# Opening of a fused attention and MoE kernel: order of the second head's rows, the transfers and the second pair's preparation

## The chip, the cores and the metric

One core of a Trainium2 chip runs the whole program. The metric is device time in microseconds of that core for one execution. Engines: TensorE (PE in rows, its weight loads PEld), VectorE (DVE), ScalarE (ACT), GpSimd (POOL) and SyncE (SP, which here issues every transfer). Each runs its own list of instructions in the order in which the program emits them, and waits on semaphores for the others.

## The reference

Clustered attention, then two feed-forward layers. Only the attention matters here. Each query and key is assigned to the nearest of 16 centroids of its head (largest cosine), and a query attends only to the keys of its own cluster:

```python
q_assign = np.argmax(np.einsum('bhsd,hcd->bhsc', q_n, c_n), axis=-1)
k_assign = np.argmax(np.einsum('bhsd,hcd->bhsc', k_n, c_n), axis=-1)
mask = q_assign[:, :, :, None] == k_assign[:, :, None, :]
scores = np.where(mask, scale * np.matmul(q, k.transpose(0, 1, 3, 2)), -1000000000.0)
scores = scores - np.max(scores, axis=-1, keepdims=True)
attn = np.exp(scores)
attn = attn / (np.sum(attn, axis=-1, keepdims=True) + 1e-09)
x = np.matmul(attn, v)
```

Batch 2, 8 heads, 768 positions, 64 values per head, float32. Behind it stand `x @ w_in`, a leaky ReLU, `@ w_out`, a norm, a gated layer and `@ w_out`.

## The kernel before

Heads go in pairs, numbered pr = 0 to 7; a pair's 768 queries go in two halves, so there are 16 phases (ph) of six slots each, one slot for each tile of 128 keys. Slot 0 is the first with score products; negative slots are the opening. A table of events, filled by `plan`, gives each step a slot and an order number in it; `slot` emits the steps of a slot sorted by that number, and this emission order is the order on every engine. Ahead of the slots runs `setup`, whose steps are put in order by the string `CHAIN`: one letter is one step (`c`, `n` the norm chains of centroids and pair 0 on VectorE, `m` the cluster products, `a` scale and argmax, `d` and `o` transfers and one-hots, `v` the rests of pair 0, `w` a run of filler products that nobody reads, their numbers in `WARM`, `l` loads of pair 1, `q` and `t` its squares and their sums).

A pair is prepared in these steps. Loads of q and k twice, row-wise (`nat`) and transposed (`raw`). `prep_sq` on ScalarE and `prep_ss` give the sums of squares, for pairs 1 to 3 on GpSimd. `prep_norm` turns them into reciprocal norms by fourteen small VectorE instructions for pair 1, and for pair 2 mostly on GpSimd. `prep_sims` part 0 multiplies raw values with centroids (L396) and part 1 transposes the result (L406) into PSUM. `prep_scale` (L413, VectorE) reads it from there, and `prep_arg` finds the largest in five steps, the last of which writes one-hot columns `oh` (L435). `prep_oht` transposes these (L444) into the single PSUM buffer `ps_pr`, ScalarE copies them out (L445), and `prep_dma_oh` sends 16 rows for each head into `op1` (L488). `prep_hi` (ScalarE, L465) and `prep_lo` (L471, VectorE for pair 0, GpSimd else) split raw values into a rounded part and a rest in `stages`; `prep_dma_a` and `prep_dma_b` send these to the operands: `op1` rows 0 to 63 hold the rounded parts, 64 to 79 the one-hots (a factor of -2^60 on one side makes other clusters vanish), 80 to 127 and `op2` the rests and, in two rows, the negated maximum.

For pair 0, head 0's one-hot rows are made straight in place: `oht_direct(0)` (twelve small products, L456, two copies by ScalarE, L459 and L460); head 1's go by `prep_oht` and `prep_dma_oh(1)`, the first transfer of slot -12.

Every phase needs the row maxima first: `max_tile` (two products on `op1` rows 0 to 79, L507, into `ps_mx`, in phase 0 also `ps_pv`; one VectorE reduction, L511), six to a phase, three for each head. `max_split` (L516, L517, VectorE) splits and negates, `max_rows` (L532) transposes, ScalarE copies the rows into `op2` (L541). Then `st_tile` makes a score tile (L554 on `op1`, L555 on `op2`, exponential on ScalarE, L556) and `pv_tiles` multiplies with v and sums (L570, L584). PSUM buffers: three `ps_st`, one `ps_mx`, one `ps_pv`, one `ps_pr`; whoever takes a buffer again waits for its last reader, also for one emitted later on another engine.

Around the change the order is: phase 0's maxima in slots -12 to -7, pair 1's sims (part 0) at the end of slot -7, its rounding and norm chain in slot -6, sims part 1 in slot -4, scale in slot -1, argmax steps and phase 1's maxima in slots 0 to 4, its one-hot transposes in slot 4, pair 2's sims in slots 4 and 5, its scale in slot 6, and the maxima of pair 1's first phase (`max_tile(2, 0)`) from slot 7.

Of the kernel before, what the change touches and what calls it, by code (L numbers as in the profile page):

```python
# [12 lines left out]
AF = mybir.ActivationFunctionType  # L13
# [5 lines left out]
BIG = float(2.0 ** 60)  # L19
# [43 lines left out]
    "hi": ((-18, 2.5), (-18, 2.6)),  # L63
    "lo": ((-10, 4.5), (-9, 4.5)),
    "sims": ((-19, 8), (-16, 1.5)),
    "norm": tuple((-18, 9 + n / 100) for n in range(14)),
    "scale": ((-13, 5),),
    "arg": ((-12, 5), (-11, 5), (-10, 5), (-10, 5.1), (-9, 5)),
    "oht": ((-8, 2.6),),
# [13 lines left out]
STEADY = 20  # L83
# [3 lines left out]
WARM = (6, 10, 1, 1, 3)  # L87
# [63 lines left out]
WARMS = ((-4, 0.3, 2),)  # L151
CHAIN = "cccwccbbccccclcsscncncncnmnnnnmnnwnnnndllxlaaaxaaawxpvvowowqqtt"
# [29 lines left out]
class Attention:  # L182
# [46 lines left out]
    def setup(self):  # L229

        nc, C, H, D = self.nc, self.C, self.H, self.D
        n = H * C
# [3 lines left out]
        src = self.centroids.rearrange("h c d -> (h c) d")  # L236
# [20 lines left out]
        v = nc.vector  # L257
# [20 lines left out]
        for i in range(2):  # L278
# [19 lines left out]
            "o": [lambda: self.oht_direct(0), lambda: self.prep_oht(0)],  # L298
# [3 lines left out]
            "v": [lambda i=i: self.prep_lo(0, i) for i in range(2)],  # L302
# [144 lines left out]
    def oht_direct(self, h):  # L447

        nc, X = self.nc, self.T // 2
        ps = [b()[0:32].rearrange("p a b -> p (a b)") for b in (self.bk.mx, self.bk.pv)]  # L450
        cols = self.oh[0].rearrange("p x e c i g -> p x (e c) i g")
        for i in (1, 0):
            for g in range(2):
                for x in range(X):
                    t = g * X + x
                    nc.tensor.matmul(ps[i][:, t * 128:(t + 1) * 128], lhsT=cols[:, x, :, i, g], rhs=self.idr,  # L456
                                     start=True, stop=True)
        o1 = self.op1[h][64:80]
        nc.scalar.copy(out=o1[:, 1, :], in_=ps[1][:16, :self.S])  # L459
        nc.scalar.activation(out=o1[:, 0, :], in_=ps[0][:16, :self.S], func=AF.Identity, scale=-BIG)  # L460
# [16 lines left out]
    def prep_dma_b(self, h):  # L477
        pr, r = h // 2, 64 * (h % 2)
        o1, o2 = f(self.op1[h % 4]), f(self.op2[h % 4])
        st = f(self.stages[pr % 2])  # L480
        d = self.nc.sync.dma_start
        d(out=o1[80:128], in_=st[r:r + 48, 0:2])
        d(out=o2[0:64], in_=st[r:r + 64, 2:4])
        d(out=o2[66:82], in_=st[r + 48:r + 64, 0:2])
# [147 lines left out]
    def plan(self):  # L632
# [3 lines left out]
        def at(s, o, fn, *a):  # L636
            ev.setdefault(s, []).append((o, len(ev.get(s, [])), fn, a))
# [4 lines left out]
        for pr in range(self.NP):  # L642
# [9 lines left out]
            if pr == 0:  # L652
                at(-12, -2, self.prep_dma_oh, 1)
                at(-12, -1, self.prep_dma_b, 0)
                at(-12, 1, self.prep_dma_b, 1)
            elif pr == 1:
                at(-5, 12, self.prep_dma_a, h)
                at(-4, 12, self.prep_dma_a, h + 1)
                at(4, 2.8, self.prep_dma_oh, h)
                at(4, 2.8, self.prep_dma_oh, h + 1)  # L660
                at(4, 12, self.prep_dma_b, h)
                at(5, 12, self.prep_dma_b, h + 1)
            else:
                for e in range(2):
                    at(b - 12, 2.5, self.prep_dma_a, h + e)
                    at(b - 12, 2.5, self.prep_dma_oh, h + e)
                    at(b - 11 + e, 2.5, self.prep_dma_b, h + e)
        for ph in range(NF):
# [3 lines left out]
            for k, s in enumerate(slots):  # L672
                at(s, 2.7 if s in slots[:k] else 0.5 if s % 2 or s < 0 else 1.5 if s < STEADY else 1.01, self.max_tile, ph, k)
# [504 lines left out]
```

## Time and profile before

| | us |
|---|---|
| three timed runs | 868.97, 876.44, 876.71 |
| their median | 876.44 |
| profiled execution | 869.91 |
| its span | 868.0 |
| TensorE, VectorE, ScalarE, GpSimd busy | 835.7, 602.4, 327.7, 395.8 |
| mean granted TensorE clock (1.00 is 2.4 GHz) | 0.992 |

The span runs from the first to the last instruction of the profiled execution; the execution's own time is 1.91 longer. Times in rows count from the start of the span. "Busy" is the time in which an engine works on instructions; the text behind "<-" in square brackets is the idle time ahead of an instruction and what the profile takes for its releaser. Of a wait for several semaphores it names the last by its own reckoning; where that one had long been done, it was another, often a transfer.

### The profile page before, as it was taken

The numbers are of one execution on the slowest core, as the hardware profiler recorded it, in microseconds if no ns is written. First come the engines' busy times: TensorE is split into PE (matmuls) and PEld (weight loads), VectorE is DVE, ScalarE is ACT, GpSimd is POOL, SyncE is SP. The second block draws the span as 40 slices with busy tenths as digits, with TensorE's granted clock in tenths as the row PEclk, the third lists the DMA queues.
The fourth block names the chain that finished last, engine by engine and source line by source line (L and its number), as shares of the span: only waits on it lengthen the run. The fifth ranks groups of instructions, "written<-read, shape, count | busy, mean of one in ns | idle before, by whom it ended". The sixth has DMA issues, their size and how long they took to land.

```text
span 868.0 us, 11480 instructions
## 1 busy us (share of the span) xinstructions
PE 835.7 (96%) x4279; PEld 633.2 (73%) x4279; DVE 602.4 (69%) x924; ACT 327.7 (38%) x623; POOL 395.8 (46%) x349
## 2 busy tenths in 40 slices
PE   5898999999999999999999999999999999999998
PEld 3554666666655688887778888778888888888886
DVE  7857787786677448999899876987555555555523
ACT  4545565565444424333344334342222122122110
POOL 4652112211002616777777665444554554554511
PEclk9799999999999999999999999999999999999999
DMA  7878076347442202222221221000221221221012
GB/s 231 213 191 205 18 197 141 113 118 161 87 123 74 74 1 71 76 75 96 73 96 53 74 71 49 24 25 26 73 72 49 74 73 49 73 73 50 0 49 97
DMA packets 24279, 75.69 MB, mean 87 GB/s; under 512 B 3680, under 2 KB 4896, under 8 KB 24224
## 3 DMA queue, kind: packets, MB, share of 16 engines
q1 hardware_dynamic: 24224, 74.96, 30.1%
q8 instruction: 34, 0.56, 0.3%
q14 instruction: 21, 0.17, 0.1%
HBM read 51.46 MB, written 3.15 MB: 63 GB/s over the span
## 4 chain that ended last, share of the span: by engine, by line
PE 72%; DVE 19%; issue 3%; ACT 2%; POOL 1%; DMA 1%; SPq 0%; DVEq 0%; ACTq 0%; POOLq 0%
PE ps_st L829 24%; PE ps_mx L829 10%; PE ps_pv L829 9%; PE ps_pv L570 7%; PE ps_pr L829 5%; PE ps_mx L507 4%; DVE dec_a L808 3%; DVE mx L511 3%; PE ps_pv L584 3%; PE ps_st L554 3%; PE ps_st L555 3%; DVE x L936 2%; DVE dec_a L806 2%; PE ps_pr L613 1%; DVE dec_e L811 1%
## 5 line engine op out<-in xcount | busy, mean ns | idle before, releaser
L892 POOL TENSOR_TENSOR gl<-v,gh 128x512 fp32r<-128x512 f32 x68 | 93.5, 1375 | 104.1 <-ACT gh L891 102.8
L556 ACT ACTIVATE p<-ps_st 128x384 f32<-128x384 f32 x192 | 85.0, 494 | 106.5 <-PE ps_st L555 105.7
L511 DVE TENSOR_REDUCE mx<-ps_mx 128x1 f32<-128x768 f32 x93 | 88.7, 954 | 43.4 <-PE ps_mx L507 42.8
L891 ACT CAST gh<-v 128x512 fp32r<-128x512 f32 x68 | 42.3, 622 | 134.3 <-DVE v L888 79.9
L888 DVE TENSOR_TENSOR v<-ps_st,t 128x512 f32<-128x512 f32 x36 | 24.9, 691 | 85.4 <-PE ps_st L829 85.4
L630 POOL TENSOR_TENSOR x1l<-X,x1h 128x384 fp32r<-128x384 f32 x15 | 16.0, 1064 | 148.7 <-ACT x1h L627 145.1
L570 PE MATMUL ps_pv<-p,vnat 128*64 128x384 f32 x384 | 72.8, 500 | 0.0
L507 PE MATMUL ps_mx<-op 80*128 80x384 f32 x186 | 56.8, 387 | 12.4 <-DVE mx L511 11.9
L884 DVE SCALAR_TENSOR_TENSOR v<-v,alpha,t 128x512 f32<-128x512 f32 x45 | 46.9, 1043 | 30.7 <-ACT v L883 30.7
L554 PE MATMUL ps_st<-op 128*128 128x384 f32 x192 | 67.8, 353 | 0.0
L829 PE MATMUL ps_st<-x1h,stage 128*128 128x512 f32 x272 | 67.8, 390 | 0.0
L808 DVE SCALAR_TENSOR_TENSOR dec_a<-raw,dec_a 128x512 uint32<-128x512 uint32 x66 | 66.1, 1002 | 2.3
L555 PE MATMUL ps_st<-op 82*128 82x384 f32 x192 | 65.4, 341 | 0.0
L936 DVE TENSOR_TENSOR x<-ps_mx,x 128x1024 f32<-128x1024 f32 x36 | 43.8, 1218 | 31.1 <-PE ps_mx L829 31.1
L816 POOL TENSOR_TENSOR dec_a<-dec_a,woh 128x512 f32<-128x512 f32 x28 | 45.5, 1623 | 36.1 <-ACT woh L819 32.3
L507 PEld LDWEIGHTS ps_mx<-op 80*128 80x128 f32 x186 | 29.0, 192 | 43.2 <-DVE mx L511 21.8
L829 PEld LDWEIGHTS ps_st<-x1h,stage 128*128 128x128 f32 x272 | 50.8, 188 | 10.6 <-ACT x1h L978 0.2
L829 PE MATMUL ps_st<-x1h,wvh 128*128 128x512 f32 x144 | 56.1, 389 | 0.0
L829 PE MATMUL ps_st<-x1h,wvl 128*128 128x512 f32 x144 | 56.1, 389 | 0.0
L829 PE MATMUL ps_st<-x1h,wih 128*128 128x512 f32 x132 | 51.7, 391 | 0.0
L829 PE MATMUL ps_st<-x1h,wil 128*128 128x512 f32 x132 | 51.4, 389 | 0.0
L811 DVE TENSOR_SCALAR dec_e<-dec_a 128x512 uint32<-128x512 uint32 x66 | 48.7, 737 | 2.2
(253 smaller groups left out, 1988.2 us busy)
## 6 DMA issues: line engine op xcount, KB each, us to landing
raw<-in_moe_w_out_dram SPq DMA_DIRECT2D x28, 512.0 KB, 3.5
op<-stage SPq DMA_DIRECT2D x32, 384.0 KB, 5.5
raw<-in_moe_w_in_dram SPq DMA_DIRECT2D x15, 512.0 KB, 3.6
raw<-in_moe_w_val_dram SPq DMA_DIRECT2D x12, 512.0 KB, 3.5
raw<-in_moe_w_gate_dram SPq DMA_DIRECT2D x12, 512.0 KB, 3.4
op<-stage SPq DMA_DIRECT2D x16, 288.0 KB, 5.8
nat<-in_qn_dram SPq DMA_DIRECT2D x8, 384.0 KB, 4.9
nat<-in_kn_dram SPq DMA_DIRECT2D x8, 384.0 KB, 5.7
```

What stands on the lines that cost most here:

```text
L507: nc.tensor.matmul(ps[:, g, :self.HS], lhsT=o1[0:80, 0, t * 128:(t + 1) * 128], rhs=o1[0:80, 1, sl], start=True, stop=True)
L511: nc.vector.tensor_reduce(out=self.mx[ph][:, k:k + 1], in_=ps[:, :, :self.HS], op=ALU.max, axis=AX.XY)
L554: nc.tensor.matmul(ps, lhsT=o1[:, 1, ks], rhs=o1[:, 0, qs], start=True, stop=False)
L555: nc.tensor.matmul(ps, lhsT=o2[:, 1, ks], rhs=o2[:, 0, qs], start=False, stop=True)
L556: nc.scalar.activation(out=self.P[s][:, e], in_=ps, func=AF.Exp, scale=self.scale)
L570: nc.tensor.matmul(ps[64 * e:64 * e + 64], lhsT=self.vnat[ph // 2][:, e, t0 + y], rhs=P[y][:, e], start=t0 + y == 0, stop=t0 + y == T - 1)
L808: v.scalar_tensor_tensor(out=a, in0=top, scalar=0xC0000000, in1=a, op0=ALU.bitwise_and, op1=ALU.bitwise_or)
L811: v.tensor_scalar(out=e, in0=a, scalar1=0xFF800000, scalar2=None, op0=ALU.bitwise_and)
L829: self.nc.tensor.matmul(ps, lhsT=a, rhs=b, start=first and i == 0, stop=last and i == len(terms) - 1)
L884: nc.vector.scalar_tensor_tensor(out=v, in0=v, scalar=self.nalpha[:, a], in1=t, op0=ALU.mult, op1=ALU.add)
L892: nc.gpsimd.tensor_tensor(out=lo, in0=v, in1=f(hi), op=ALU.subtract)
L936: nc.vector.tensor_tensor(out=dst, in0=ps, in1=dst, op=ALU.add)
```

## The change

`CHAIN` puts two loads of pair 1 (instead of one) ahead of pair 0's operand transfers, moves one `v` (the rest of k, now `prep_lo(0, 1)` first) into the norm chain, adds `e` behind `d` (the two parts of `prep_dma_b` that need only the rest of k) and `f` behind the second `v` (the part that needs the rest of q), and puts the other two loads of pair 1 behind the one-hots. `oht_direct` is called for both heads, with 16 columns each; for head 1 it takes three `ps_st` buffers and `ps_pr` and four copies on ScalarE. `WARM` and `WARMS` give other filler products: 13 for 10, 3 for 1, and two in each of the slots -10 to -7 for two in slot -4. `SECOND`, the table of pair 1, moves rounding, sims, norm chain, scale, argmax and one-hot transposes to later slots (0 to 5); its transfers move accordingly. In phase 1 the maximum products stand behind the score products of their slot.

```diff
 SECOND = {
-    "hi": ((-18, 2.5), (-18, 2.6)),
+    "hi": ((-12, 4), (-11, 4)),
     "lo": ((-10, 4.5), (-9, 4.5)),
-    "sims": ((-19, 8), (-16, 1.5)),
-    "norm": tuple((-18, 9 + n / 100) for n in range(14)),
-    "scale": ((-13, 5),),
-    "arg": ((-12, 5), (-11, 5), (-10, 5), (-10, 5.1), (-9, 5)),
-    "oht": ((-8, 2.6),),
+    "sims": ((-12, 1.4), (-11, 1.7)),
+    "norm": tuple((-12, 9 + n / 100) for n in range(14)),
+    "scale": ((-11, 5),),
+    "arg": ((-10, 5), (-10, 5.1), (-9, 5), (-9, 5.1), (-8, 5)),
+    "oht": ((-7, 2.6),),
...
-WARM = (6, 10, 1, 1, 3)
+WARM = (6, 13, 1, 3, 3)
...
-WARMS = ((-4, 0.3, 2),)
-CHAIN = "cccwccbbcccccclcsscncncncnmnnnnmnnwnnnndllxlaaaxaaawxpvvowowqqtt"
+WARMS = ((-10, 0.3, 2), (-9, 0.3, 2), (-8, 0.3, 2), (-7, 0.3, 2))
+CHAIN = "cccwccbbcccccllcsscncncncnmnnnvnmnnwnnnndexaaaxaaawxwpvfowollqqtt"
...
+            "e": [lambda: [self.prep_dma_b(h, (0, 2)) for h in range(2)]],
+            "f": [lambda: [self.prep_dma_b(h, (1,)) for h in range(2)]],
-            "o": [lambda: self.oht_direct(0), lambda: self.prep_oht(0)],
+            "o": [lambda: self.oht_direct(0), lambda: self.oht_direct(1)],
...
-            "v": [lambda i=i: self.prep_lo(0, i) for i in range(2)],
+            "v": [lambda i=i: self.prep_lo(0, i) for i in (1, 0)],
...
     def oht_direct(self, h):
...
+        if h:
+            hi = [self.bk.st(), self.bk.pr()]
+            ps = [[self.bk.st(), self.bk.st()], hi]
+        else:
+            ps = [b().rearrange("p a b -> p (a b)") for b in (self.bk.mx, self.bk.pv)]
+            ps = [[b, b[:, self.HS:]] for b in ps]
...
-                    nc.tensor.matmul(ps[i][:, t * 128:(t + 1) * 128], lhsT=cols[:, x, :, i, g], rhs=self.idr,
-                                     start=True, stop=True)
+                    nc.tensor.matmul(ps[i][g][0:16, x * 128:(x + 1) * 128], lhsT=self.oh[0][:, x, h, :, i, g],
+                                     rhs=self.idr, start=True, stop=True)
...
-        nc.scalar.copy(out=o1[:, 1, :], in_=ps[1][:16, :self.S])
-        nc.scalar.activation(out=o1[:, 0, :], in_=ps[0][:16, :self.S], func=AF.Identity, scale=-BIG)
+        for i in (1, 0):
+            parts = [(ps[i][g][:16, :self.HS], o1[:, i, sl]) for g, sl in self.halves()] if h else \
+                [(ps[i][0][:16, :self.S], o1[:, i, :])]
+            for src, dst in parts:
+                if i:
+                    nc.scalar.copy(out=dst, in_=src)
+                else:
+                    nc.scalar.activation(out=dst, in_=src, func=AF.Identity, scale=-BIG)
...
-    def prep_dma_b(self, h):
+    def prep_dma_b(self, h, parts=(0, 1, 2)):
...
+        pairs = ((o1[80:128], st[r:r + 48, 0:2]), (o2[0:64], st[r:r + 64, 2:4]), (o2[66:82], st[r + 48:r + 64, 0:2]))
+        for i in parts:
+            self.nc.sync.dma_start(out=pairs[i][0], in_=pairs[i][1])
...
             if pr == 0:
-                at(-12, -2, self.prep_dma_oh, 1)
-                at(-12, -1, self.prep_dma_b, 0)
-                at(-12, 1, self.prep_dma_b, 1)
+                pass
             elif pr == 1:
-                at(-5, 12, self.prep_dma_a, h)
-                at(-4, 12, self.prep_dma_a, h + 1)
-                at(4, 2.8, self.prep_dma_oh, h)
-                at(4, 2.8, self.prep_dma_oh, h + 1)
-                at(4, 12, self.prep_dma_b, h)
-                at(5, 12, self.prep_dma_b, h + 1)
+                at(1, 12, self.prep_dma_a, h)
+                at(1, 12.1, self.prep_dma_a, h + 1)
+                at(5, 2.8, self.prep_dma_oh, h)
+                at(5, 2.8, self.prep_dma_oh, h + 1)
+                at(5, 12, self.prep_dma_b, h)
+                at(6, 12, self.prep_dma_b, h + 1)
...
-                at(s, 2.7 if s in slots[:k] else 0.5 if s % 2 or s < 0 else 1.5 if s < STEADY else 1.01, self.max_tile, ph, k)
+                at(s, 2.7 if s in slots[:k] else 0.5 if (s % 2 or s < 0) and ph != 1 else 1.5 if s < STEADY else 1.01, self.max_tile, ph, k)
```

In `SECOND` a slot is counted from 12: (-12, 1.4) is slot 0, (-7, 2.6) is slot 5.

## Rows read from the trace of the kernel before

**Rows 1.** Page, the chain that ended last: share of the span by engine

```profile
PE 72%; DVE 19%; issue 3%; ACT 2%; POOL 1%; DMA 1%; SPq 0%; DVEq 0%; ACTq 0%; POOLq 0%
```

**Rows 2.** Busy time by stretch; columns: us, engines' busy (instructions), clock, transfers

```profile
0.00:88.00 88.00, 69.36 (x407) 41.14 (x407) 63.58 (x144) 41.42 (x78) 39.93 (x106) 0.92 0.79 208
88.00:868.00 780.00, 766.33 (x3875) 592.07 (x3873) 538.79 (x780) 286.30 (x545) 355.83 (x243) 1.00 0.25 74
18.86:21.27 2.41, 0.00 (x0) 0.00 (x0) 1.44 (x4) 0.00 (x0) 2.02 (x7) 0.64 0.95 177
21.27:25.80 4.53, 4.48 (x18) 2.18 (x18) 3.27 (x6) 0.47 (x1) 2.49 (x6) 0.50 0.95 203
25.80:29.90 4.10, 4.10 (x14) 3.20 (x14) 3.08 (x15) 3.62 (x7) 0.00 (x0) 0.51 1.01 279
38.40:46.60 8.20, 7.53 (x43) 4.02 (x43) 5.70 (x12) 3.29 (x7) 7.00 (x14) 0.79 0.25 75
66.00:69.00 3.00, 1.00 (x10) 0.57 (x12) 2.52 (x5) 1.68 (x4) 1.45 (x3) 1.00 0.56 114
```

**Rows 3.** Timeline, TensorE, 21 to 29 us; columns: start, length, instructions

```profile
21.30 0.98 PE L507 MATMUL ps_pv<-op 80*128 80x384 f32 x2 [2.44 <-DVE mh L517]
...
24.27 1.51 PE L396 MATMUL ps_st<-raw,cb 128*32 128x384 f32 x8
...
27.63 0.67 PE L554 MATMUL ps_st<-op 128*128 128x384 f32 x1
...
28.74 0.52 PE L555 MATMUL ps_st<-op 82*128 82x384 f32 x1
```

**Rows 4.** Timeline and transfers issued, 17 to 18 us: KB each, us to landing

```profile
17.16 0.63 SPq L488 DMA_DIRECT2D op<-oht  x1
...
op<-oht SPq DMA_DIRECT2D x1, 96.0 KB, 4.1
```

**Rows 5.** Timeline, VectorE, 14 to 39 us

```profile
14.64 1.82 DVE L471 TENSOR_TENSOR stage<-raw,stage 128x768 fp32r<-128x768 f32 x2
...
17.23 0.96 DVE L511 TENSOR_REDUCE mx<-ps_mx 128x1 f32<-128x768 f32 x1 [0.76 <-PE ps_mx L507]
...
20.20 0.17 DVE L517 SCALAR_TENSOR_TENSOR mh<-mx,mh 128x3 fp32r<-128x3 f32 x1
...
25.65 0.17 DVE L337 TENSOR_SCALAR n_a<-ss 128x24 int32<-128x24 int32 x1
...
28.47 0.30 DVE L344 RECIPROCAL n_a<-n_y 128x24 f32<-128x24 f32 x1
...
35.74 1.73 DVE L517 SCALAR_TENSOR_TENSOR mh<-mx,mh 128x3 fp32r<-128x3 f32 x1
...
37.40 0.94 DVE L511 TENSOR_REDUCE mx<-ps_mx 128x1 f32<-128x768 f32 x1
```

**Rows 6.** Timeline, ScalarE, GpSimd and VectorE, 29 to 50 us

```profile
29.68 0.83 ACT L366 ACTIVATE nat<-nat 128x768 f32<-128x768 f32 x1
...
30.59 3.02 POOL L377 TENSOR_TENSOR nat<-nat 128x384 f32<-128x384 f32 x5 [6.44 <-ACT nat L366]
...
33.86 3.59 POOL L471 TENSOR_TENSOR stage<-raw,stage 128x768 fp32r<-128x768 f32 x2
...
48.11 0.23 POOL L328 TENSOR_TENSOR n_y<-n_y,n_a 128x24 f32<-128x24 f32 x1
...
49.22 0.56 DVE L413 TENSOR_TENSOR sims<-ps_pr,n_a 128x384 f32<-128x384 f32 x1
```

**Rows 7.** Timeline, 45 to 51 us, and transfers issued near 47 us

```profile
45.94 0.58 ACT L445 ACTIVATE oht<-ps_pr,ohs 128x384 fp32r<-128x384 f32 x1 [2.25 <-PE ps_pr L444]
...
47.56 0.52 PE L406 MATMUL ps_pr<-idf,simc 128*128 128x128 f32 x3
...
op<-oht SPq DMA_DIRECT2D x2, 96.0 KB, 3.1
...
50.93 0.61 PE L507 MATMUL ps_mx<-op 80*128 80x384 f32 x2
```

More of the change, by code (lines that the diff above doesn't have):

```diff
@@ L150 @@
 LATE = (1,2)
-WARMS = ((-4, 0.3, 2),)
-CHAIN = "cccwccbbccccclcsscncncncnmnnnnmnnwnnnndllxlaaaxaaawxpvvowowqqtt"
+WARMS = ((-10, 0.3, 2), (-9, 0.3, 2), (-8, 0.3, 2), (-7, 0.3, 2))
+CHAIN = "cccwccbbcccccllcsscncncncnmnnnvnmnnwnnnndexaaaxaaawxwpvfowollqqtt"
 LINE = 32
@@ L449, in oht_direct @@
         nc, X = self.nc, self.T // 2
-        ps = [b()[0:32].rearrange("p a b -> p (a b)") for b in (self.bk.mx, self.bk.pv)]
-        cols = self.oh[0].rearrange("p x e c i g -> p x (e c) i g")
+        if h:
[4 more added lines that the diff above has]
+            ps = [[b, b[:, self.HS:]] for b in ps]
         for i in (1, 0):
@@ L454, in oht_direct @@
                 for x in range(X):
-                    t = g * X + x
-                    nc.tensor.matmul(ps[i][:, t * 128:(t + 1) * 128], lhsT=cols[:, x, :, i, g], rhs=self.idr,
-                                     start=True, stop=True)
+                    nc.tensor.matmul(ps[i][g][0:16, x * 128:(x + 1) * 128], lhsT=self.oh[0][:, x, h, :, i, g],
+                                     rhs=self.idr, start=True, stop=True)
         o1 = self.op1[h][64:80]
-        nc.scalar.copy(out=o1[:, 1, :], in_=ps[1][:16, :self.S])
-        nc.scalar.activation(out=o1[:, 0, :], in_=ps[0][:16, :self.S], func=AF.Identity, scale=-BIG)
+        for i in (1, 0):
[6 more added lines that the diff above has]
+                    nc.scalar.activation(out=dst, in_=src, func=AF.Identity, scale=-BIG)
     def prep_hi(self, pr, i):
@@ L480, in prep_dma_b @@
         st = f(self.stages[pr % 2])
[L481 to L484, printed above, removed]
+        pairs = ((o1[80:128], st[r:r + 48, 0:2]), (o2[0:64], st[r:r + 64, 2:4]), (o2[66:82], st[r + 48:r + 64, 0:2]))
+        for i in parts:
+            self.nc.sync.dma_start(out=pairs[i][0], in_=pairs[i][1])
     def prep_dma_oh(self, h):
```

## The prediction

> **What bounds the kernel now.** I read the page first, its chain: TensorE carries 72% of it and VectorE 19% [rows 1]. Then the busy time by stretch. From 88 us on TensorE is busy 766.3 of 780 us at full clock; in the first 88 us it stands still for 18.6 us and the granted clock is 0.92 [rows 2]. The change touches the preparation of pairs 0 and 1, so its worth is read in the first 51 us. My mark is the first maximum product of pair 1, `max_tile(2, 0)`, at 50.93 us [rows 7]: behind it every engine but the transfer queue keeps its order, so what is won or lost by then is carried to the end.
>
> Next the timeline of the opening, engine by engine. TensorE has one hole, 18.86 to 21.27 [rows 2]. The profile names a vector instruction as the releaser of the product behind it [rows 3], but that product is the first that reads head 1, whose one-hot rows come by a transfer issued at 17.16 that lands 4.1 us later, at 21.26 [rows 4]: that is the true releaser. In and behind the hole the granted clock falls to 0.5, the 1.2 GHz level, and stays there to the end of the next two stretches, near 29.8 [rows 2]. In this slow time stand pair 1's cluster products (1.51 us) and two fillers, all ahead of the first score product at 27.63; the fourth ends at 29.26 [rows 3].
>
> VectorE has little rest meanwhile: reductions of 0.96, pair 1's norm chain (fourteen small instructions, 25.65 to 28.77, 3.1 us), then argmax steps between phase 1's reductions. One tiny instruction, the second half of a split, takes 1.73 us where 0.17 is usual: it starts while GpSimd holds one of two subtractions of 1.8 us (33.86 to 37.45). The reduction behind it, phase 1's fourth, ends at 38.34 [rows 5, 6]. GpSimd itself works nearly without a gap from 30.59 to 48.34 at pair 2's norms; only then VectorE finishes these and scales, 49.22 to 49.78 [rows 6].
>
> **The change part by part.** All sums run against the profiled execution: 869.91 us, a span of 868.0 and 1.91 around it. The timed runs are 868.97, 876.44 and 876.71; their median stands 6.53 above the profiled one.
>
> *Rest of k early.* One of two subtractions (1.82 for both [rows 5]) moves into pair 0's norm chain; the one-hots, at that chain's end, come 0.9 later. Four transfers (786 KB) now leave before q's rest is ready and two (786 KB) behind it. The 786 KB ahead of them had landed when the first reduction ran at 17.23 [rows 5]; the other 1.57 MB at the 203 GB/s seen behind the hole [rows 2] take 7.7 us, so all is there by 25.0 at the latest. The scores won't ask before 25.4 (below): covered, by little at worst. Pair 1's raw rows and the values go behind these six; they are needed from 26.3 on. I put the transfers at nothing; if the rate were a fifth lower, the scores would be up to 1.5 late, which the wait found below still covers.
>
> *Head 1 without a transfer.* The 2.41 us hole goes. TensorE gets six more fillers and twelve small products ahead of the first maximum tile in place of three transposes; ScalarE four half-row copies. Head 0 needs now only two of the four one-hot steps before its products start, which gives some of the 0.9 back. I take the first reduction as 0.8 late, 18.05 (bounds: nothing, and 1.8, the 0.9 twice). Four copies of at most 0.58 (a copy of 384 columns on 128 rows [rows 7]) have head 1's rows there before the fourth reduction. Six reductions of 0.96, two splits of 0.4 and gaps of 0.3: end at 24.9. Before, the norm chain began behind them at 25.65. Won so far: 0.75.
>
> *Pair 1 behind the first scores.* Between the last split and the scores stand only three small products and a short copy: first score product at 25.4, fourth ending at 26.3 against 29.26. Won: 3.0. The eight fillers stand in waits for reductions, at no cost there.
>
> *Where that goes.* VectorE did pair 1's norm chain while TensorE made the slow products. Now it idles from 24.9 until scores, cluster products (0.8, half of 1.51 at full clock) and a maximum tile are through, 27.7, and does the chain behind that reduction: reduction to 28.65, chain 3.1 and 0.5 for GpSimd beside it, 32.3; second reduction 33.25; 0.65 for the product and third to 34.9; the split meets GpSimd's subtractions as before, 37.3; fourth reduction 38.25. Before: 38.34 [rows 5]. The win is gone by here. Bounds of the 0.5: nothing, and 3.2, the whole of GpSimd's adds (30.59 to 33.8 before [rows 6]).
>
> A rule is weighed here. The row shows 1.73 for 0.17, but the same instruction at 20.20 took 0.17 beside GpSimd's adds [rows 5]. The Trainium skill, GPSIMD Engine Reference, section 1 Specifications, says that GpSimd shares its SBUF interfaces with VectorE and contends with instructions of two SBUF inputs, which most of the chain's are. By that rule for all of them the sum would be up to 2.7 higher, 874.8; by the row it is 872.1.
>
> *One-hot transposes of pair 1.* They move from slot 4 to slot 5, behind the sims transposes of pair 2. Both write `ps_pr`, of which there is one buffer, and pair 2's sims stay in it until VectorE's scale in slot 6. Before, the order was the other way round, and the scale at 49.22 held up nobody. TensorE gets there at 45.2: before, 9.74 us lay between the fourth reduction's end and the end of the same sims transposes (38.34 to 48.08 [rows 5, 7]); 1.1 of it were pair 1's transposes and copy (0.52, 0.58), and a clock of 0.79 over 8.2 us [rows 2] means 3.4 at half clock, 1.7 owed to it; 38.25 + 9.74 - 2.8. How early is the scale? ScalarE's squares of pair 2, behind the first scores, end at 29.35 (30.51 before). GpSimd's run of 17.75 then ends at 47.15; 0.25 for its wait on VectorE's argmax steps; VectorE's rest of the norms and the scale took 1.44 (48.34 to 49.78 [rows 6]): 48.8, 1.0 earlier than before. Then transposes 0.5, ScalarE's copy 0.6, and the transfer, 3.1 from issue to landing [rows 7]: 53.1. Behind the waiting transposes stand a score pair and a pv group; from the copy's end to the mark 4.4 us passed before, with these two and more in them [rows 7], so from 49.3 they are through by 53.1 too. Before, the transfer left at the copy's end, 46.5, and landed at 49.6, hidden by 1.3. The other transfers that leave later are needed at slot 12, some 20 us on.
>
> Sum at the mark: 53.1 - 50.93 = 2.2 late; 869.9 + 2.2 = 872.1.
>
> **The rivals.** *The win is kept* (faster). GpSimd comes through earlier, or TensorE doesn't wait for the scale. For it: TensorE gets to the transposes 2.9 ahead of before (45.2 against 48.08). Against: GpSimd's nearly gapless run [rows 6]. Time: 869.9 - 2.9 = 867.0.
>
> *Moved, not won* (no change). The scores start earlier, VectorE's chain takes it back, and TensorE comes so late to the transposes that the scale and the transfer are mostly covered: 869.9, within 1.
>
> *The clock* (slower). Two new waits of TensorE, for the norm chain (about 30.1 to 33.3) and for the scale (45.2 to 48.8), are longer than the 2.41 after which 0.5 was granted to 29.8 [rows 2]. It decides if both are answered like that. From 21.27 to 29.90 TensorE was busy 8.58 us at half clock, 4.3 owed to it; twice that, less a little that hides behind VectorE: 872.1 + 8 = 880. Against: from 66 to 69 TensorE was busy 1.0 of 3 us and kept its clock [rows 2]. The Trainium skill, TensorE: Matmul & The Clock Gate, section What's actually happening, has the slow clock as the default and activity as what releases it; by that rule this rival, with which the hole agrees and 66 to 69 doesn't.
>
> **How the numbers follow.** The wait behind the scale is an order that the code fixes; its size rests on GpSimd's measured run: 0.47. Kept win 0.20, moved 0.18, clock 0.15. The likeliest gives 872.1, its own range is 870 to 875 (the contention's bounds, a landing 0.6 off). Over the cases the range is 866 (the kept win, with 1 to spare) to 881 (the clock's case, likewise); it takes in most of the runs' own spread, by whose upper two the sum would be 878.7. Against the median of 876.44, faster by over 1% is below 867.7, slower above 885.2; 1% is about what a measurement of this kernel can tell. The first needs the kept win and an execution like the profiled one: 0.17. The second needs the clock's full price on an execution like the upper two: 0.05. Within 1%: 0.78.
>
> **What would show it.** Right: no hole before the fourth maximum tile; first score product near 25.4; VectorE idle to about 27.7, the norm chain behind phase 1's first reduction; the fourth reduction near 38; TensorE idle before the one-hot transposes (L444) until VectorE's scale (L413); the mark near 53. Wrong: L444 without that wait; a split of 0.2 in phase 1; GpSimd through before 46; or long stretches at 0.5 after 30, the clock's case.

## The result, and the profile after

The changed kernel takes 883.19 us (median of four executions, 879.65 to 885.44) against 874.88 for the kernel before, run beside it (median of four, 868.97 to 876.71). The ratio is 1.0113, with a 95% interval of 1.0068 to 1.0158: slower, by 8.3 us between the medians and by about 10 by the ratio. The forecast was 872.1 in a range of 866 to 881; it is wrong, on the slow side, and the number lies nearest to that of the rival called the clock. In one kernel further down (both orders mended, fewer fillers) a single execution took 1855.5 us; its ratio leaves it out. The profiled execution took 885.44 us with a span of 883.7. In the code after, the lines of [rows 3 to 7] stand two to ten lower: the maximum's product L507 is L517, its reduction L511 is L521, the norm chain is L333 to L346, scores L564 and L565, one-hot transposes L446, the scale L415.

Busy time by stretch of the kernel after, with the columns of [rows 2]:

```profile
0.00:88.00 88.00, 67.69 (x332) 40.17 (x334) 57.42 (x130) 35.64 (x67) 37.87 (x106) 0.83 0.63 170
12.00:14.00 2.00, 2.00 (x7) 1.52 (x6) 1.86 (x5) 0.00 (x0) 0.00 (x0) 1.00 0.98 226
29.90:46.80 16.90, 11.65 (x41) 6.75 (x38) 11.92 (x21) 6.39 (x11) 10.79 (x15) 0.50 0.44 123
46.80:57.00 10.20, 7.29 (x49) 3.81 (x47) 7.98 (x18) 4.04 (x9) 4.66 (x13) 1.00 0.00 0
57.00:63.90 6.90, 5.88 (x23) 2.50 (x23) 0.86 (x2) 1.56 (x3) 0.00 (x0) 0.51 0.39 79
81.00:87.60 6.60, 5.93 (x24) 3.72 (x26) 3.08 (x6) 3.17 (x6) 0.72 (x1) 0.50 0.80 165
88.00:883.70 795.70, 780.07 (x3971) 599.52 (x3967) 548.56 (x795) 292.97 (x559) 357.49 (x244) 1.00 0.26 76
```

All the loss lies in the first 88 us (the prediction meant to read it in the first 51): behind them the clock is full and TensorE busy 98% of the time, before and after, and VectorE's reductions of the row maxima, matched one by one, stand 15.2 us behind those of the kernel before at 100 us and 15.6 at the last one. What is new in this execution is three stretches at half clock (0.50, the 1.2 GHz level), 30.4 us in all; before there were 10.2 us near 20 to 30 and a shorter one near 40 to 44 [rows 2].

TensorE's timeline of the kernel after:

```profile
11.69 5.53 PE L314 MATMUL ps_st<-zero,idr 128*128 128x512 f32 x14
...
28.16 0.39 PE L564 MATMUL ps_st<-op 128*128 128x384 f32 x1
...
40.50 1.01 PE L517 MATMUL ps_mx<-op 80*128 80x384 f32 x2 [5.25 <-DVE mx L521]
...
58.02 0.62 PE L446 MATMUL ps_pr<-idr,oh 128*128 128x128 f32 x3 [3.35 <-DVE sims L415]
...
64.08 0.61 PE L517 MATMUL ps_mx<-op 80*128 80x384 f32 x2
```

The last line is the mark: 64.08 in place of 50.93 [rows 7], 13.15 late. Two waits of TensorE stand ahead of it, one for VectorE's second reduction of phase 1 (5.25) and one for pair 2's scale (3.35). VectorE's timeline of the same execution says where the first comes from:

```profile
20.66 0.96 DVE L521 TENSOR_REDUCE mx<-ps_mx 128x1 f32<-128x768 f32 x1 [3.72 <-PE ps_mx L517]
...
31.31 0.96 DVE L521 TENSOR_REDUCE mx<-ps_mx 128x1 f32<-128x768 f32 x1 [3.50 <-PE ps_mx L517]
32.18 0.17 DVE L339 TENSOR_SCALAR n_a<-ss 128x24 int32<-128x24 int32 x1
...
32.60 0.91 DVE L333 TENSOR_TENSOR n_a<-n_y,ss 128x24 f32<-128x24 f32 x1
...
35.70 1.85 DVE L344 TENSOR_TENSOR n_y<-n_y,ss 128x24 f32<-128x24 f32 x1
37.58 1.72 DVE L345 TENSOR_SCALAR n_y<-n_y 128x24 f32<-128x24 f32 x1
39.33 0.30 DVE L346 RECIPROCAL n_a<-n_y 128x24 f32<-128x24 f32 x1
...
46.68 0.96 DVE L521 TENSOR_REDUCE mx<-ps_mx 128x1 f32<-128x768 f32 x1 [2.41 <-PE ps_mx L517]
```

and GpSimd's beside it:

```profile
32.47 2.94 POOL L379 TENSOR_TENSOR nat<-nat 128x384 f32<-128x384 f32 x5 [3.91 <-ACT nat L368]
...
35.70 3.56 POOL L482 TENSOR_TENSOR stage<-raw,stage 128x768 fp32r<-128x768 f32 x2
...
51.05 0.23 POOL L327 TENSOR_TENSOR n_a<-n_y,ss 128x24 f32<-128x24 f32 x1 [7.01 <-DVE n_y L341]
```

Pair 1's fourteen small instructions now run from 32.18 to 39.63, 7.4 us, where they took 3.1 [rows 5]. Two of them, 0.18 each elsewhere, take 1.85 and 1.72 while GpSimd holds its two subtractions of 1.8. The fourth reduction of phase 1 then starts at 46.68 (37.40 before), VectorE comes late to the two small steps that open pair 2's norms, and GpSimd stands idle for 7.01 us behind them; before it worked there nearly without a gap [rows 6].

### The profile page after: what moved, and what is told of

Read it like the earlier page. It is cut to its first block, busy times and chain, and to the rows that moved or that the text cites. A ratio compares the mean times of both kernels' runs of the same rounds, so it can differ in the third digit from the quotient of the medians.

```text
span 883.7 us, 11520 instructions
## 1 busy us (share of the span) xinstructions
PE 847.8 (96%) x4299; PEld 639.7 (72%) x4299; DVE 606.0 (69%) x924; ACT 328.6 (37%) x626; POOL 395.4 (45%) x349
## 4 chain that ended last, share of the span: by engine, by line
PE 73%; DVE 19%; issue 3%; ACT 2%; POOL 2%; DMA 1%; SPq 0%; DVEq 0%; ACTq 0%; POOLq 0%
PE ps_st L837 24%; PE ps_mx L837 10%; PE ps_pv L837 9%; PE ps_pv L580 7%; PE ps_pr L837 5%; PE ps_mx L517 5%; DVE mx L521 3%; DVE dec_a L816 3%; PE ps_pv L594 3%; PE ps_st L564 3%; PE ps_st L565 3%; DVE x L944 2%; DVE dec_a L814 2%; PE ps_pr L623 1%; DVE dec_e L819 1%
## 5 line engine op out<-in xcount | busy, mean ns | idle before, releaser
L521 DVE TENSOR_REDUCE mx<-ps_mx 128x1 f32<-128x768 f32 x93 | 88.7, 953 | 59.4 <-PE ps_mx L517 59.0
L580 PE MATMUL ps_pv<-p,vnat 128*64 128x384 f32 x384 | 75.5, 515 | 0.0
L517 PE MATMUL ps_mx<-op 80*128 80x384 f32 x186 | 58.3, 395 | 14.3 <-DVE mx L521 13.7
L564 PE MATMUL ps_st<-op 128*128 128x384 f32 x192 | 68.9, 359 | 0.0
L565 PE MATMUL ps_st<-op 82*128 82x384 f32 x192 | 66.3, 345 | 0.0
L517 PEld LDWEIGHTS ps_mx<-op 80*128 80x128 f32 x186 | 29.3, 196 | 48.3 <-DVE mx L521 24.7
```

Of the source, the lines that this page charges most:

```text
L517: nc.tensor.matmul(ps[:, g, :self.HS], lhsT=o1[0:80, 0, t * 128:(t + 1) * 128], rhs=o1[0:80, 1, sl], start=True, stop=True)
L521: nc.vector.tensor_reduce(out=self.mx[ph][:, k:k + 1], in_=ps[:, :, :self.HS], op=ALU.max, axis=AX.XY)
L564: nc.tensor.matmul(ps, lhsT=o1[:, 1, ks], rhs=o1[:, 0, qs], start=True, stop=False)
L565: nc.tensor.matmul(ps, lhsT=o2[:, 1, ks], rhs=o2[:, 0, qs], start=False, stop=True)
L580: nc.tensor.matmul(ps[64 * e:64 * e + 64], lhsT=self.vnat[ph // 2][:, e, t0 + y], rhs=P[y][:, e], start=t0 + y == 0, stop=t0 + y == T - 1)
```

## Experiments

Theory after this first reading: two orders of the change cost the time, the norm chain's place beside GpSimd's work and the one-hot transposes behind the scale, and the clock multiplies both. Rivals: the front half (rest of k early, head 1 without a transfer, fillers) costs it; or the chain is long for another reason than GpSimd.

**The front half alone.** `SECOND`, pair 1's transfers and the maxima's order numbers as before, all else as changed:

```diff
...
-    "norm": tuple((-12, 9 + n / 100) for n in range(14)),
-    "scale": ((-11, 5),),
...
-    "oht": ((-7, 2.6),),
...
+    "norm": tuple((-18, 9 + n / 100) for n in range(14)),
+    "scale": ((-13, 5),),
...
+    "oht": ((-8, 2.6),),
...
```

> Only the front half of the change: the rest of k early, head 1's one-hots without a transfer, the new fillers; pair 1's table and its transfers as in the kernel before. Theory A (the cost lies in pair 1's move, that is VectorE's norm chain behind the first reduction and the one-hot transposes behind pair 2's scale): about the kernel before or better, 866 to 872, the mark (first maximum product of pair 1) at 48 to 51 us. Theory B (the cost lies in the front: 16 fillers and 24 small products in TensorE's list ahead of the first maximum tile, at half clock early on): slower than before by 2 to 4 us, the first reduction near 19 to 20.7 instead of 17.2. Theory C (the clock alone): like the kernel before but with its spread.

875.12 us against 873.79, ratio 1.0010 (0.9989 to 1.0031). No measurable loss, and no gain either: its first reduction starts at 18.02 and its first score product at 27.27, only 0.4 before [rows 3], and its mark stands at 50.97, where it was. So the 8 us come from pair 1's orders, or from their meeting with the front.

**The two orders, singly and together.** Each edit is made to the changed kernel:

```diff
-    "oht": ((-7, 2.6),),
+    "oht": ((-7, 1.65),),
```

> The changed kernel with one number other: pair 1's one-hot transposes stand ahead of pair 2's sims transposes in slot 5, so they no longer wait for pair 2's scale. If that wait costs what the trace shows (3.35 us of TensorE, and the transfer behind it): the mark at 58 to 59 instead of 64.1, total 4 to 6 us less than the changed kernel, 877 to 879. If the wait is only filled by another (VectorE's late argmax): 1 us less or nothing.

```diff
-    "norm": tuple((-12, 9 + n / 100) for n in range(14)),
+    "norm": tuple((-18, 9 + n / 100) for n in range(14)),
```

> The changed kernel with VectorE's norm chain of pair 1 back ahead of phase 1's first reduction (slot -6); all else as changed. If the chain's place is the cause (7.4 us from 32.2 to 39.6 beside GpSimd, where 3.1 are usual): chain of about 3.1 us, phase 1's fourth reduction near 41 instead of 47.6, total 4 to 6 us less than the changed kernel. If GpSimd's run sets the end anyway (pair 2's norms): the reductions come earlier but the scale of pair 2 hardly, 1 to 2 us less.

And both edits at once:

> Both edits together. If the two causes add up: 8 to 11 us less than the changed kernel, 872 to 875, level with the kernel before. If they are one cause (the same slack counted twice): no better than the better one alone. If the front is to blame: still 4 us or more above the kernel before.

The times, all against the same 873.79: one-hot transposes ahead of the scale 882.19, 1.0087 (1.0060 to 1.0113); norm chain ahead of the scores 879.30, 1.0054 (1.0032 to 1.0075); both 874.99, 1.0006 (0.9986 to 1.0027). From the changed kernel's 1.0113 the transposes alone win 2.3 us (0.0026 of 874; 4 to 6 were expected), the chain alone 5.2, both 9.4: the two orders together account for the loss. The interval of the changed kernel is 4 us to either side, so the first of these wins can't be told from nothing. The three variants, measured side by side, tell more: with the other order mended the chain's place is worth 7.2 us (882.19 to 874.99) and the transposes 4.3 (879.30 to 874.99). That the chain weighs more is likely, not certain (1.0087 and 1.0054, with intervals that overlap), and whether the two add up stays open.

With the chain ahead of the scores, VectorE's timeline (first and last of the fourteen), then TensorE's:

```profile
28.23 0.18 DVE L339 TENSOR_SCALAR n_a<-ss 128x24 int32<-128x24 int32 x1 [0.78 <-POOL ss L379]
...
31.05 0.30 DVE L346 RECIPROCAL n_a<-n_y 128x24 f32<-128x24 f32 x1
```

```profile
51.86 0.45 PE L446 MATMUL ps_pr<-idr,oh 128*128 128x128 f32 x3 [3.00 <-DVE sims L415]
```

3.1 us again, since GpSimd has nothing to do then; the wait behind the scale is still there, 3.00. With the transposes moved alone, VectorE and TensorE:

```profile
33.12 1.67 DVE L345 TENSOR_SCALAR n_y<-n_y 128x24 f32<-128x24 f32 x1
```

```profile
49.56 0.42 PE L446 MATMUL ps_pr<-idr,oh 128*128 128x128 f32 x3 [0.43 <-DVE oh L437]
```

the wait behind the scale is gone, and the chain still long (5.7 us). With both edits, TensorE's timeline:

```profile
47.03 0.42 PE L446 MATMUL ps_pr<-idr,oh 128*128 128x128 f32 x3
...
51.62 0.62 PE L517 MATMUL ps_mx<-op 80*128 80x384 f32 x2
```

neither wait, and the mark is back within 0.7 of before.

**Is it the subtractions, or any work of GpSimd?** In the changed kernel the subtractions of pair 1 and pair 2 on GpSimd are put off by a slot:

```diff
 SECOND
-    "lo": ((-10, 4.5), (-9, 4.5)),
+    "lo": ((-9, 4.4), (-9, 4.5)),
 THIRD
-    "lo": ((-22, 4.5), (-20, 4.5)),
+    "lo": ((-21, 4.5), (-20, 4.5)),
```

> The changed kernel with one thing moved: GpSimd's three subtractions of pair 1 and 2 that stood in slot 2 go to slot 3, behind the squares' sums, so that VectorE's norm chain, still behind phase 1's first reduction, no longer meets them. If meeting GpSimd is what stretches the chain (7.4 us for 3.1): chain 3.3 to 4.5 us, phase 1's second reduction 3 us earlier, total 2 to 4 us less than the changed kernel (879 to 881), unless the subtractions then meet the split. If only the place of the chain counts: chain as long as before the edit, total as the changed kernel, 883.

879.15 us, 1.0078 (1.0051 to 1.0105) against 872.89. VectorE's and GpSimd's timelines:

```profile
29.92 0.92 DVE L333 TENSOR_TENSOR n_a<-n_y,ss 128x24 f32<-128x24 f32 x1
...
33.04 1.03 DVE L344 TENSOR_TENSOR n_y<-n_y,ss 128x24 f32<-128x24 f32 x1
```

```profile
29.80 2.96 POOL L379 TENSOR_TENSOR nat<-nat 128x384 f32<-128x384 f32 x5 [3.86 <-ACT nat L368]
...
33.03 2.83 POOL L379 TENSOR_TENSOR nat<-nat 128x384 f32<-128x384 f32 x5
```

With the subtractions out of the way, the second sum of squares took their place, and the chain still takes 5.1, more than the 3.3 to 4.5 expected. Where it stands, some work of GpSimd runs beside it. The time is 3 us under the changed kernel's by the ratios, which the two intervals don't tell from nothing.

**GpSimd's work put beside the chain of the kernel before.** This takes the change away altogether. Behind pair 1's second sum of squares the kernel before gets spare work on GpSimd, with results that nothing reads:

```diff
+        if i == 1 and pr == 1:
+            q, k = (self.nat[pr][:, j].rearrange("p t h d -> p (t h d)") for j in range(2))
+            for _ in range(3):
+                self.nc.gpsimd.tensor_tensor(out=k, in0=q, in1=k, op=ALU.subtract)
```

> The kernel before, with three subtractions more on GpSimd (128x768, two operands from SBUF, results that nothing uses) right behind the second sum of squares of pair 1, so that they run beside the norm chain (25.65 to 28.77 before) from about 24.2 to 29.7. Theory (two-operand work of GpSimd stretches VectorE's small instructions): the chain takes 5 to 6.5 us in place of 3.1, the second phase's first reduction and pair 1's scale move by as much, single instructions of 0.18 take 0.5 to 1.8; the time rises by 1 to 3 us, since the mark follows this chain. Rival (the chain in the changed kernel is long from its place, VectorE's own queue or the throttled TensorE): the chain stays at 3.1 to 3.6 and the time within 1 us.

and in its sibling four instructions with one operand from SBUF:

```diff
-            for _ in range(3):
-                self.nc.gpsimd.tensor_tensor(out=k, in0=q, in1=k, op=ALU.subtract)
+            for _ in range(4):
+                self.nc.gpsimd.tensor_scalar(out=k, in0=q, scalar1=-0.5, scalar2=1.5, op0=ALU.mult, op1=ALU.add)
```

> The same place with four multiply-adds on GpSimd in place of the three subtractions: 128x768 with one operand from SBUF and two constants. If it is the second SBUF operand that stretches VectorE: the chain stays at 3.1 to 3.4 and the time within 1 us of before. If any access of GpSimd to SBUF does it: the chain takes 4 us or more, much as with the subtractions.

With the subtractions the time was 877.92 us against 872.15, 1.0049 (1.0021 to 1.0077); with the multiply-adds 873.62, 1.0013 (0.9991 to 1.0036). VectorE and GpSimd with the subtractions (in both kernels the split is L520 and L521):

```profile
25.77 1.71 DVE L521 SCALAR_TENSOR_TENSOR mh<-mx,mh 128x3 fp32r<-128x3 f32 x1
...
27.60 1.79 DVE L339 TENSOR_SCALAR n_y<-n_a 128x24 int32<-128x24 int32 x1
...
29.64 1.70 DVE L332 SCALAR_TENSOR_TENSOR n_a<-n_a,n_y 128x24 f32<-128x24 f32 x1
```

```profile
25.66 5.65 POOL L384 TENSOR_TENSOR nat<-nat 128x768 f32<-128x768 f32 x3
32.33 2.85 POOL L377 TENSOR_TENSOR nat<-nat 128x384 f32<-128x384 f32 x5 [1.02 <-ACT nat L366]
```

and with the multiply-adds:

```profile
26.15 0.67 DVE L521 SCALAR_TENSOR_TENSOR mh<-mx,mh 128x3 fp32r<-128x3 f32 x1
...
26.94 0.82 DVE L339 TENSOR_SCALAR n_y<-n_a 128x24 int32<-128x24 int32 x1
...
28.01 0.69 DVE L332 SCALAR_TENSOR_TENSOR n_a<-n_a,n_y 128x24 f32<-128x24 f32 x1
```

```profile
25.03 3.65 POOL L384 TENSOR_SCALAR nat<-nat 128x768 f32<-128x768 f32 x4
```

Three instructions of GpSimd at 1.88 each, and three of VectorE held for 1.7 to 1.8; four at 0.91, and three held for 0.7 to 0.8. So a VectorE instruction that is caught waits for about what is left of one GpSimd instruction, then none or one slips through before the next is caught. The chain takes 7.2 us (27.40 to 34.61, of it 1.0 beside the kernel's own sums from 32.33 on) in the first and 4.3 in the second. The guess that only a second operand of GpSimd's does it falls: one is enough, and the hold is as long as its instructions are, in these two lengths. GpSimd's own later work can't be what costs the time, since GpSimd stands idle for 1.02 us behind the spare work until ScalarE's squares are there. So GpSimd's work beside the small instructions is enough to cost time: the kernel before, with that and nothing else, loses 2 to 7 us, more than the 1 to 3 expected. It is not the whole price of the chain's place in the changed kernel: there the chain's own 3.1 us also stand between two reductions, and no run left it there with GpSimd idle beside it. By the traces 2.6 to 4.3 us of the chain are the hold (5.7 and 7.4 less 3.1); that is an estimate of its share, not a measured one.

**The fillers.** The prediction put them at no cost. In the front half alone, and in the kernel with both orders mended, the fillers of before came back:

```diff
-WARM = (6, 13, 1, 3, 3)
+WARM = (6, 10, 1, 1, 3)
-WARMS = ((-10, 0.3, 2), (-9, 0.3, 2), (-8, 0.3, 2), (-7, 0.3, 2))
+WARMS = ((-4, 0.3, 2),)
```

(the second kernel has the first pair of lines only):

> The front half alone with the fillers of the kernel before (5 fewer ahead of the one-hots, none between phase 0's maxima, two in slot -4). Theory A (the fillers in TensorE's list cost time by themselves and give it back through a higher clock, so that front_only ended level): the mean granted clock falls from about 0.992 to 0.988, the first reduction comes 1 to 2 us earlier, and the total stays within 1 us of front_only (875) or of the kernel before (874). Theory B (the fillers are free): same marks, total 1 to 3 us more than front_only because the clock is lower. Theory C (fillers are pure cost): total 2 to 4 us less than front_only, 871 to 873.

> The kernel with both orders put back (both_first), with 5 fewer fillers ahead of the one-hots, the eight between phase 0's maxima kept. Theory A: first reduction 1 to 2 us earlier, clock as in both_first (0.991), total 872.5 to 874. Theory B (free): same as both_first, 875. Theory C: 871 to 873.

and the kernel before got those of the changed one (the same diff, reversed):

> The kernel before with the fillers of the changed kernel (five more in the preparation's order, eight in place of two among the first max products) and nothing else. Theory (the fillers cost about as much as the clock gives back): the first reduction 0.5 to 1 later than 17.23, the mark within 1 us of 50.93, the mean granted clock over the runs near 0.991 in place of 0.988, the time within 2 us of before. Prediction's term (eight fillers cost nothing): the mark as before, the time 1 to 2 us under before. Rival: they hold TensorE where max products and scores wait, the mark 1 to 2 later without a higher clock, the time 2 to 4 us above.

The ratios are 1.0021 (0.9995 to 1.0046), 1.0023 (0.9997 to 1.0050) and 1.0004 (0.9987 to 1.0021): none can be told from before. Two effects may hide in that. Over the executions of one kernel the span grows as the mean granted clock falls, by 6.1 us for each 0.01 (a fit through 219 executions, each about its own kernel's mean). Held at a clock of 0.99 by that fit, which makes the following estimates, the kernel before stands at a span of 870.2, with the fillers at 872.1; the front half at 874.1 with all fillers and at 871.6 with few. By that, all the added fillers together cost 1.9 to 2.5, and they raise the mean clock from 0.9882 to 0.9911 and from 0.9876 to 0.9918, which gives 1.8 to 2.5 back. This is not shown: a clock that is raised where TensorE waits anyway would look the same in the fit, and the mark shows no cost. The same fit puts the front half with few fillers 1.4 above the kernel before, so the front itself wins nothing.

In the kernel before with fillers the mark hardly moves, though much ahead of it does:

```profile
26.21 0.41 PE L554 MATMUL ps_st<-op 128*128 128x384 f32 x1 [0.65 <-DMA op<-stage]
...
28.33 0.66 PE L555 MATMUL ps_st<-op 82*128 82x384 f32 x1 [1.71 <-DMA op<-stage]
...
50.96 0.62 PE L507 MATMUL ps_mx<-op 80*128 80x384 f32 x2
```

Here the order of transfers of before does show: score products that come a little earlier wait for the rest of k, 0.65 and 1.71. In the changed kernel no score waits for a transfer; that part of it does what it was taken to do.

**Two tries at a version that beats both.** First, the kernel with both orders mended and fewer fillers, with pair 1's scale, argmax steps, one-hot transposes and their transfers each about a slot earlier:

```diff
-    "sims": ((-12, 1.4), (-11, 1.7)),
+    "sims": ((-12, 1.4), (-11, 1.03)),
...
-    "scale": ((-11, 5),),
-    "arg": ((-10, 5), (-10, 5.1), (-9, 5), (-9, 5.1), (-8, 5)),
-    "oht": ((-7, 1.65),),
+    "scale": ((-11, 1.2),),
+    "arg": ((-11, 5), (-10, 5), (-10, 5.1), (-9, 5), (-9, 5.1)),
+    "oht": ((-8, 2.6),),
...
```

> A try at a kernel better than both: front half with 5 fewer fillers, pair 1's cluster products behind the first scores, but VectorE's norm chain ahead of phase 1's reductions, scale and argmax one slot earlier and the one-hot transposes in slot 4 as in the kernel before. If the front's 3 us survive once no wait stands in the way: the mark at 47 to 49, total 870 to 872. If VectorE's work in phase 1 and the split beside GpSimd set the pace: mark near 51, total as both_first, 874 to 875.

The time was 874.37 us, 1.0018 (0.9997 to 1.0038). Then head 1's direct transposes behind the first two maximum products and pair 1's squares, too:

```diff
-CHAIN = "...xwpvfowollqqtt"
+CHAIN = "...xwpvfowllqqtt"
...
             if pr == 0:
-                pass
+                at(-12, 0.6, self.oht_direct, 1)
```

> The kernel early_arg with the second head's direct one-hot transposes and copies behind the first two max products and behind the squares of pair 1. Theory (what is left of the front's price is that head 1's work stands ahead of the first max products, 0.7, and of the squares, 2.4): the first reduction at 17.9 instead of 18.62, GpSimd's sums done by 24.5 instead of 26.55, the norm chain from 25.5 to 28.6, the mark 50.5 to 51.0 instead of 51.51; the time 0.5 to 2 us under early_arg, 873 to 874 as before, perhaps under it. Rival (the slots of the loop set what follows): the front moves and the mark stays at 51.5; the time stays at 874.4.

It took 875.29 us, 1.0028 (1.0010 to 1.0045), above the kernel before and not under the first try as hoped. In its profile the front moves as hoped: first reduction 17.72, norm chain 25.86 to 28.97, the mark at 50.19, 0.74 ahead of before. Yet its span is 873.0 against 868.0. Busy time by stretch behind the mark, first that kernel, then the kernel before:

```profile
68.00:76.00 8.00, 7.83 (x35) 3.97 (x35) 4.75 (x8) 2.71 (x6) 2.77 (x2) 0.59 0.84 175
84.00:92.00 8.00, 7.38 (x33) 3.52 (x33) 3.38 (x6) 2.32 (x5) 0.00 (x0) 0.57 0.29 113
```

```profile
68.00:76.00 8.00, 6.98 (x48) 3.97 (x47) 5.98 (x10) 4.31 (x10) 2.78 (x2) 1.00 0.84 176
84.00:92.00 8.00, 8.00 (x58) 4.45 (x59) 5.51 (x12) 3.79 (x9) 0.76 (x1) 1.00 0.39 147
```

The order there is the same in both, but in the one TensorE gets 35 and 33 products done at a clock near 0.6 where the other does 48 and 58 at full clock. What is won or lost by the mark is not carried to the end untouched: this execution, with two more slow stretches, lost 5.7 us behind the mark, and by 100 us all but 0.4 of it. Over twelve profiled kernels, the changed one among them, the distance to the kernel before grew by 0 to 5.4 us between the mark and 100 us and by at most 0.5 behind that. The profiled execution of the kernel before, with no slow stretch behind 44 us, is a good one: of the hundred executions of that kernel measured beside the experiments one had a shorter span, and their mean is 871.3. No version ran faster than the kernel before.

## Why the prediction was wrong, point by point

The step that failed is the price of the norm chain's new place: 0.5 us for GpSimd beside it, in a chain of 3.6, where the chain took 7.4 and GpSimd's part was 4.3. The mechanism, small instructions held beside GpSimd, had been named, bounded at 3.2 and set aside. The wait for the scale came as forecast.

*Rest of k early, transfers at nothing.* Held: no score waits for a transfer, and the run with fillers in the kernel before shows what the old order would have cost.

*First reduction 0.8 late, at 18.05.* In the profiled execution it started at 20.66, 2.6 later than that. The one-hot columns were there no later than in the kernel with both orders mended (from 15.10 on, against 15.45), but TensorE came to the direct products at 17.86, against 16.06: 1.8 of the 2.6. Its first fourteen fillers took 5.53 us from 11.69 on, seven in the two microseconds from 12 to 14 where the kernel with both orders mended did eleven:

```profile
12.00:14.00 2.00, 2.00 (x11) 1.63 (x10) 1.88 (x5) 0.00 (x0) 0.00 (x0) 1.00 0.98 223
```

The 1.00 of the clock column is no reading there. The trace's record of the granted clock begins at 16.1 us in the profiled execution of the changed kernel and at 10.5 in the other, and the column counts time without a record as full. The fillers show the level: up to 16.1 they start 0.43 us apart, behind it 0.23, so TensorE ran near half clock until then. In thirteen profiled executions that moment lies between 5.9 us (the kernel before) and 16.1, in no order by kernel: the late start belongs to this execution, not to the change. The chain-first variant started like that as well (20.29, record from 15.2); the front half alone had 18.02, the other variants of the changed kernel 17.7 to 18.9, and for those the term is near.

*The 2.41 hole goes; first score at 25.4, 3.0 won.* The hole is gone in every variant with the direct rows. With the transposes mended the first score stood at 25.28, so the step is right; in the profiled execution the late start put it at 28.16. Of the fillers "at no cost" the runs show that in sum they change nothing (1.0004, 0.9987 to 1.0021).

*VectorE idles until the first reduction of phase 1, then does the chain in 3.1 + 0.5.* The place was right (idle 3.50, chain right behind that reduction). The 0.5 is the term that failed: 4.3 in the profiled execution, 2.6 with the transposes moved, 2.0 with the subtractions away. No row gives the 0.5; it was set between one split caught by a subtraction and another that went free beside the adds [rows 5]. The upper bound, 3.2 for all of the adds, left out that the two subtractions follow them and that a chain that runs late meets both. The trace of the kernel before held two more instructions caught by subtractions, VectorE first and then GpSimd (the other subtractions are in [rows 6]):

```profile
34.49 1.22 DVE L516 TENSOR_SCALAR mh<-mx 128x3 fp32r<-128x3 f32 x1
...
40.90 1.79 DVE L337 TENSOR_SCALAR n_a<-ss 128x24 int32<-128x24 int32 x1
```

```profile
40.83 1.82 POOL L471 TENSOR_TENSOR stage<-raw,stage 128x768 fp32r<-128x768 f32 x1
```

By these rows, each subtraction of 1.8 beside the chain could cost up to 1.6. The Trainium skill, GPSIMD Engine Reference, section 1 Specifications, warns of contention between GpSimd and VectorE on their SBUF interfaces; it was weighed and priced at 2.7, and set aside. The runs agree with it: L344, with two inputs, took 1.85. L345, with one, took 1.72; the prediction had left out the two-port performance modes that the same row of the page names, and no run shows in which mode L345 ran. That the split at 20.20 went free shows only that not every instruction is caught.

*The fourth reduction ends at 38.25.* It ended at 47.64. Of the 9.4 the late start gives 2.6 and the chain 3.8 (7.4 less the 3.6 of the sum). The remaining 3.0 came mostly with the clock: at 0.50 from 29.9 to 46.8 the pv group ahead of the fourth product took 2.83 us for what takes 1.51 at full clock in the same trace.

*One-hot transposes behind the scale: TensorE waits from 45.2 to 48.8.* The mechanism held with its size: 3.35 measured for 3.6, released by the scale, from 54.7 to 58.0 instead, because all was late by then; GpSimd's run, taken as gapless, had the 7.01 of idle time in it. The mark came 11.0 behind the forecast of 53.1: 9.2 by the scale (58.0 for 48.8) and 1.8 in what follows it, at a clock of 0.51. Its price at the mark was put at 2.2; undone with the chain early it is worth 4.3 us of the time.

*The clock, a rival at 0.15 and 880.* Its sign came in the profiled execution, and its number came near, but that is luck: two of the four executions had a mean granted clock of 0.992 and 0.994 and still spans of 879.6 and 877.9, against 867.2 to 871.2 for the 23 executions of the kernel before at these two clocks. At an equal clock of 0.99 the fit puts the changed kernel at 879.6 and the kernel before at 870.2 (estimates), 9.4 apart, as much as the whole loss. Against the kernel with both orders mended, which has the same fillers, 2 of the 8 us may be the clock's (0.9875 against 0.9910, by the fit, from four executions). The rival was put down to two new waits; but in the profiled execution the first slow stretch starts at 29.9, before the wait for the chain (35.25 to 40.50), behind a wait of 1.66 ahead of the scores (the last max product's end to 27.95), and holds through it. The second, from 57.0, does start in the wait for the scale (54.7 to 58.0), and a third near 81.0, behind a wait of 1.31 for pair 2's one-hot columns; before, the same wait, 1.33, left the clock at full. The Trainium skill, TensorE: Matmul & The Clock Gate, section What's actually happening, takes the slow clock as the default that activity releases; the first two stretches agree with it, the third is matched by one that did not come. The rival's 880 stood 3 below the median, the upper end of the range 2 below it.

*The mark decides.* Too strong. The mark was 13.15 late and the span 15.7 longer; of the other 2.5, 2.1 came by 100 us, over the stretch from 81.0. Part of the 13.15 is this execution's late start. With the mark 0.74 early, the span was 5.0 longer (the second try).

*What would show it.* Of the four signs of a wrong forecast, one appeared: long stretches at 0.5 after 30. The signs that were to confirm the steps, the hole gone, the idle VectorE, the wait released by the scale, all came; only the sizes differed.

Left open: why full clock first comes at 5.9 us in one execution and at 16.1 in another; and why the slow stretches behind the mark come in one execution and stay away in another whose instruction order there is the same.

## What to carry to other kernels

Before a chain of small VectorE instructions is moved, look at what GpSimd does beside its new place: each GpSimd instruction of 1.8 us here held one VectorE instruction of 0.2 for nearly that long, so what is added to the chain goes by the number and length of the GpSimd instructions beside it, not by its own work. A buffer with one copy makes the order of its two users a wait; ask when the earlier one's reader comes. And in the opening of a kernel whose TensorE is not yet kept busy, a gain of one microsecond is smaller than what the clock may take back, so it must be measured over many executions, and one profile should not be set against another without asking when each one's full clock began.

## What was not expected of the hardware

A VectorE instruction of 0.18 us on 128x24 elements took 1.85 beside GpSimd, and one with a single operand (L345) as much as one with two. The hold is as long as one GpSimd instruction, 1.7 to 1.8 beside 1.88 and 0.7 to 0.8 beside 0.91, and one operand of GpSimd's from SBUF is enough for it (beside four multiply-adds the chain took 4.3 for 3.1).

The start of an execution differs: full clock came at 16.1 us in the one profiled after, at 10.5 in another with the same fillers, at 5.9 in the kernel before. The clock column and the mean clock don't show it, since both count the time ahead of the record as full.

The span of one and the same kernel follows the mean granted clock of the execution: the kernel before ran from 867.2 at 0.994 to 875.7 at 0.981, and the fit leaves about a microsecond to either side.
